# The last weight quarter of a fused attention and FFN kernel in halves, and the first half of its instruction order sought anew

## The chip, the cores and the metric

The kernel runs on one NeuronCore of one Trainium2 chip. The metric is the device time of one execution in microseconds (us). Before the change three executions took 270.04, 270.14 and 270.77; the median is 270.14. Engines are named as in the profile: PE is TensorE (matrix products), DVE is VectorE, ACT is ScalarE, POOL is GpSimd, SP is SyncE, whose queue issues all loads and stores here.

## The reference

Two layers run one behind the other. The first is a linear attention over 8 batches, 8 heads, 576 positions and 64 elements per head, with a cosine and a sine weight by position; the second is a feed-forward layer on its 4608 output rows of 512:

```python
q_p = phi(q, cos_w, sin_w)          # relu(x)*cos and relu(x)*sin, side by side: 128 features
k_p = phi(k, cos_w, sin_w)
kv = np.einsum('bhsf,bhsd->bhfd', k_p, v)
z = np.sum(k_p, axis=2)
num = np.einsum('bhsf,bhfd->bhsd', q_p, kv)
den = np.einsum('bhsf,bhf->bhs', q_p, z)[..., None] + 1e-06
x = (num / den)                     # (8, 8, 576, 64), then to rows of 512
h = x @ w_in                        # 512 -> 2048
g = np.maximum(0.01 * h, h)
out = g @ w_out                     # 2048 -> 512
```

Inputs and output are float32; the kernel computes its products from float16 copies and adds up in float32.

## The kernel before, in words

The 4608 rows are worked off in nine groups of 512: group g (0 to 7) holds the first 512 positions of batch g, group 8 the last 64 positions of all batches. For each batch, VectorE or ScalarE build the weighted parts of k and q (`k_part`, `q_part`; `k_pair` for two heads of batches 0 and 1), cast v to float16 (`v_pair`, `v_main`, `v_tail`; the last 64 columns of each load are ones, so that the product also gives z), TensorE forms kv (`kv_half` for half of the heads in batches 0 and 1, `kv_all` later), an engine copies it out of PSUM, q's parts are transposed (on TensorE with `q_turn` and a copy `q_turned` in batches 0 and 1, by a DMA later), TensorE forms the numerator and denominator (`num_half`, `num`), and `divide` takes a small `den`, a reciprocal and a product. The result x is transposed (`x_turn` and the copy `x_turned` for groups 0 and 1, `x_transpose` for group 2, a DMA later).

The feed-forward layer's first product is plain for groups 0 and 1 (`ffn1`, `quad`, `f1_pair`), and takes seven products of half-size blocks for the others (`p1`), with sums of blocks of the weights (`w1_sums`) and of x (`x_sums`, tile `xw`) made ahead. The second product is plain for group 0 (`ffn2`: 16 matmuls of 512 columns for each of four token tiles, four for each quarter of w2) and takes seven products for the others (`p2`), with sums of w2 (`w2_sums`) and of g (`g_sums`). What the sevens leave in PSUM is put together by `u_copy`, `u_add`, `seed`, `lrelu`, and `o_copy`, `o_add`; `o_store` writes 512 KB out.

The weights come in quarters: `load_w1` and `load_w2` (line 161, 1 MB each for w2) fill staging buffers, `cast_w1` and `cast_w2` (line 570) make float16 copies. The casts and copies go through `copy` (lines 261 to 265), which takes the engine as an argument, so an operation can be on VectorE, ScalarE or GpSimd.

What sets the order: the program is built without a scheduler. Every engine runs its instructions in the order in which the Python code issues them, and waits at the head of its queue for what the next one needs. All loads go through SP's queue in the order of their issue; the same 16 DMA engines serve them. Buffers come from pools of fixed size, and a load into a buffer waits for the last reader of what it held. Up to group 0's second product and group 1's attention the order is written out as calls (lines 599 to 776). The rest are calls handed to `put` (line 1240) with a place from the table `PLACE` (line 1080); the table `ON` gives the engine; the list is sorted by place and called.

Idle matmuls on a blank tile (`idle`) keep TensorE running during the first loads.

Of the kernel before, what the change touches and what calls it, by code (L numbers as in the profile page):

```python
# [9 lines left out]
dt = mybir.dt  # L10
# [4 lines left out]
J = 4  # L15


@with_exitstack
def kernel(
# [62 lines left out]
    st = {"h_turn": 0}  # L82

    def psum(where, shape, dtype, name):
        if where == "h":
            where = f"h{st['h_turn']}"
        if where[0] == "h":
            st["h_turn"] = 1 - int(where[1])
        return ps_of[where[0]].tile(shape, dtype, name=name, tag="ps_" + where)
# [5 lines left out]
    def staged(shape, name, soon=False):  # L95
        p, tag = (early, "early") if soon else (stage, "stage")
        return p.tile(shape, dt.float32, name=name, tag=tag)

    def load_main(nm, src, b, parts=(0, 1), soon=False):

        if parts[0] == 0:
            st[nm, b] = staged([P, H, J, D], f"{nm}st", soon)
        lo, hi = 4 * parts[0], 4 * parts[-1] + 4
        nc.sync.dma_start(
            st[nm, b][:, lo:hi],
            src[b, lo:hi, 0:MAIN, :].rearrange("h (p j) d -> p h j d", j=J),
        )

    def load_kvtail(nm, src, b):

        t = kvtail.tile([P, H // 2, D], dt.float32, name=f"{nm}tl", tag="kvtail")
        v4 = src[b, :, MAIN:S, :].rearrange("(c o) p d -> o p c d", o=2)
        for o in range(2):
            nc.sync.dma_start(t[o * TAIL : (o + 1) * TAIL], v4[o])
        st[nm + "t", b] = t

    def load_qtail(i):
        if "qt" not in st:
            st["qt"] = staged([P, J, H, D], "qtl")
        for o in range(2):  # L120
            nc.sync.dma_start(
                st["qt"][o * TAIL : (o + 1) * TAIL, i],
                q[2 * i + o, :, MAIN:S, :].rearrange("h p d -> p h d"),
            )

    def load_pair(nm, src, b, lo, hi):
# [3 lines left out]
        flat = src[b].rearrange("h s d -> (h s d)").rearrange("(c x e) -> x c e", x=P, e=JP * D)  # L130
# [3 lines left out]

    def load_k(b):
        load_main("k", k, b)
        load_kvtail("k", k, b)

    def load_v(b):
        load_main("v", v, b)  # L140
        load_kvtail("v", v, b)
# [12 lines left out]
    def load_w1(i, cp):  # L154
# [6 lines left out]
    def load_w2(i):  # L161
        t = staged([P, 4, DM], "w2st", i > 1)
        nc.sync.dma_start(t, w2v[i])  # L163
        st["w2", i] = t

    load_main("q", q, 0, (0,))
    load_pair("k", k, 0, 0, 1)
    load_pair("k", k, 0, 1, 2)
    load_main("q", q, 0, (1,))
    load_pair("k", k, 0, 2, 4)  # L170
    load_pair("v", v, 0, 0, 2)
    load_pair("v", v, 0, 2, 4)
    load_w1(0, 0)
    load_w1(1, 0)
    load_w1(0, 1)
    load_w1(1, 1)
    load_w1(3, 0)
    load_w1(3, 1)
    load_w1(2, 0)
    load_w1(2, 1)  # L180

    blank = early.tile([P, MAIN], dt.float16, name="blank", tag="blank", bufs=1)
    nc.vector.memset(blank, 0.0)
    none = const.tile([P, P], dt.float16, name="none")
    nc.gpsimd.memset(none, 0.0)

    def idle(n, where="h1"):
# [4 lines left out]
    idle(11)  # L192

    ident32 = early.tile([P, P], dt.float32, name="ident32", tag="ident32", bufs=1)
    make_identity(nc, ident32)
    ident = const.tile([P, P], dt.float16, name="ident")
    nc.vector.tensor_copy(ident, ident32)
    w_ang = math.pi / 2.0 / S  # L200
    half_pi = const.tile([P, 1], dt.float32, name="half_pi")
    nc.vector.memset(half_pi, math.pi / 2.0)
    eps = const.tile([P, 1], dt.float32, name="eps")
    nc.vector.memset(eps, 1e-6)
    zero = const.tile([P, 1], dt.float32, name="zero")
    nc.vector.memset(zero, 0.0)
    NA = J + 1 + JP
    pos = const.tile([P, NA], dt.float32, name="pos")
    nc.gpsimd.iota(
        pos[:, 0:J],  # L210
        pattern=[[1, J]],
        base=0,
        channel_multiplier=J,
        allow_small_or_imprecise_dtypes=True,
    )
    for o in range(2):
        nc.gpsimd.iota(
            pos[o * TAIL : (o + 1) * TAIL, J : J + 1],
            pattern=[[1, 1]],
            base=MAIN,  # L220
            channel_multiplier=1,
            allow_small_or_imprecise_dtypes=True,
        )
        nc.gpsimd.iota(
            pos[o * TAIL : (o + 1) * TAIL, J + 1 : NA],
            pattern=[[1, JP]],
            base=0,
            channel_multiplier=JP,
            allow_small_or_imprecise_dtypes=True,
        )  # L230
    cos_t = const.tile([P, NA], dt.float32, name="cos_t")
    sin_t = const.tile([P, NA], dt.float32, name="sin_t")
    nc.scalar.activation(cos_t, pos, AF.Sin, bias=half_pi, scale=w_ang)
    nc.scalar.activation(sin_t, pos, AF.Sin, bias=zero, scale=w_ang)
    warm = const.tile([P, 1], dt.float16, name="warm")
    nc.scalar.activation(warm, zero, AF.Lrelu)

    ones = const.tile([P, H, J, 2], dt.float32, name="ones")
    nc.vector.memset(ones, 1.0)
    vmain = const.tile([P, H, J, NE], dt.float16, name="vmain")  # L240
    nc.vector.tensor_copy(vmain[:, :, :, D:NE], ones)
    vtail = const.tile([P, H // 2, 2, NE], dt.float16, name="vtail")
    nc.gpsimd.memset(vtail, 0.0)
    for o in range(2):
        sl = slice(o * TAIL, (o + 1) * TAIL)
# [671 lines left out]
    def f1_all(g):  # L917
# [16 lines left out]
        if sets == 4:  # L934
            return
# [406 lines left out]
```

## Time and profile before

| what | value |
|---|---|
| median of three executions | 270.14 us |
| span of the profiled execution | 268.3 us |
| TensorE busy | 262.5 us, 98% |
| VectorE busy | 209.2 us, 78% |
| ScalarE busy | 198.6 us, 74% |
| GpSimd busy | 7.7 us, 3% |
| bytes moved by DMA | 57.05 MB, mean 213 GB/s |

The total of the profiled execution itself is not given; the median of the others lies 1.84 us above its span. In a list of instructions the columns are start, duration (or the sum, where an entry holds several, "x4"), engine, line, operation, tile written from tiles read, and shapes; in brackets stands the idle time of the engine ahead of the instruction, and what ended it. The duration of a pipelined matmul overlaps with the next, so the pace of TensorE is read from one start to the next. The names of tiles: `qst`, `kst`, `vst`, `kpr`, `vpr`, `w1st`, `w2st` are staging buffers, `xp` and `xs` quotients, `xT` transposed x, `ps_...` PSUM tiles, `u` the sums of the first product, `ob` the output's.

### The profile page before, as it was taken

The page shows a single profiled execution, that of the slowest core. Times are in us where ns is not written, and L with a number is a line of the kernel's source. Part 1 is how long each engine was busy: PE and PEld are TensorE (multiplying, and loading weights), DVE is VectorE, ACT ScalarE, POOL GpSimd, SP SyncE. Part 2 cuts the span into 40 slices and gives each one's busy share as a digit, 9 for nine tenths or more (in the row PEclk, how much of TensorE's full clock was granted, in tenths as well). Part 3 has the DMA queues.
Part 4 walks back from the last instruction along what each step waited for, and adds up shares of the span by engine and source line. Part 5 has one row for each costly group of instructions (what it writes and reads, how often), then busy time and mean ns, then how long its engine had stood idle before and what let it go on. Part 6 is the DMA issues. An engine that isn't in the chain of part 4 may idle for free.

```text
span 268.3 us, 6694 instructions
## 1 busy us (share of the span) xinstructions
PE 262.5 (98%) x2715; PEld 222.9 (83%) x2715; DVE 209.2 (78%) x436; ACT 198.6 (74%) x336; POOL 7.7 (3%) x20
## 2 busy tenths in 40 slices
PE   8999999999999999999999999999999999999994
PEld 3585455566999999999999999999998999999983
DVE  4894998997998998889979967897876674746641
ACT  7675545787989999689878967984996666785621
POOL 2121011000000000000000000000000000000000
PEclk9999999999999999999999999999999999999999
DMA  6999999999999999989899999798893623200116
GB/s 207 377 385 399 380 411 365 276 249 281 209 304 254 234 240 245 264 199 222 221 231 238 198 293 255 140 181 151 135 204 22 138 43 125 112 2 0 78 36 201
DMA packets 82654, 57.05 MB, mean 213 GB/s; under 512 B 54464, under 2 KB 75968, under 8 KB 82112
## 3 DMA queue, kind: packets, MB, share of 16 engines
q1 hardware_dynamic: 82320, 56.37, 84.0%
q8 instruction: 21, 0.34, 0.5%
q10 hardware_dynamic: 304, 0.26, 0.3%
q14 instruction: 9, 0.07, 0.1%
HBM read 36.70 MB, written 9.44 MB: 172 GB/s over the span
## 4 chain that ended last, share of the span: by engine, by line
PE 82%; DMA 13%; SPq 3%; DVE 1%; POOL 0%; issue 0%
PE ps_o L975 34%; PE ps_h L882 18%; PE ps_s L882 14%; DMA w2st<-in_moe_w_out_dram 6%; PE ps_h L833 5%; DMA w1st<-in_moe_w_in_dram 4%; PE ps_num L418 3%; DMA kpr<-in_k_dram 3%; PE ps_kv L317 2%; SPq L131 2%; PE ps_h L975 2%; PE ps_o L543 1%; PE ps_s L975 1%; PE ps_kv L324 1%; DVE w L265 0%; SPq L163 0%
## 5 line engine op out<-in xcount | busy, mean ns | idle before, releaser
L975 PEld LDWEIGHTS <-g 128*128 128x128 f16 x640 | 62.1, 98 | 6.8
L268 DVE TENSOR_TENSOR u<-ps_s,u 128x512 f32<-128x512 f32 x56 | 38.5, 687 | 19.3 <-PE ps_s L882 18.4
L882 PEld LDWEIGHTS <-w 128*128 128x128 f16 x448 | 48.7, 114 | 1.0
L975 PE MATMUL ps_o<-w,g 128*128 128x256 f16 x352 | 46.8, 273 | 0.0
L902 ACT COPY u<-ps_h 128x512 f32<-128x512 f32 x56 | 32.8, 589 | 6.3 <-PE ps_h L882 6.0
L882 PEld LDWEIGHTS <-wa 128*128 128x128 f16 x336 | 34.4, 106 | 1.9
L882 PE MATMUL ps_h<-xw,w 128*128 128x256 f16 x224 | 32.5, 273 | 0.0
L975 PE MATMUL ps_o<-wb,g 128*128 128x256 f16 x232 | 31.5, 273 | 0.0
L909 ACT ACTIVATE g<-u 128x1024 f16<-128x1024 f32 x28 | 29.6, 1060 | 2.3 <-DVE u L268 2.3
L975 PEld LDWEIGHTS <-gs 128*128 128x128 f16 x256 | 24.6, 98 | 2.6
L994 ACT COPY ob<-ps_o 128x512 f32<-128x512 f32 (+1 forms) x32 | 18.0, 561 | 6.0 <-PE ps_o L975 5.8
L892 ACT COPY ps_s<-ps_h 128x512 f32<-128x512 f32 x28 | 16.2, 579 | 6.2 <-PE ps_h L882 5.7
L895 ACT ACTIVATE g<-ps_s 128x512 f16<-128x512 f32 x28 | 16.8, 601 | 5.1 <-PE ps_s L882 4.8
L895 ACT ACTIVATE g<-ps_h 128x512 f16<-128x512 f32 x28 | 16.7, 600 | 5.3 <-PE ps_h L882 5.1
L436 DVE TENSOR_TENSOR xs<-ps_num,rden 128x512 f16<-128x512 f32 x28 | 19.4, 691 | 1.5
L268 DVE TENSOR_TENSOR ob<-ps_o,ob 128x512 f32<-128x512 f32 (+1 forms) x22 | 14.8, 672 | 3.3 <-PE ps_o L975 2.1
L882 PE MATMUL ps_s<-xT,wa 128*128 128x256 f16 x112 | 16.8, 273 | 0.0
L882 PE MATMUL ps_h<-xw,wa 128*128 128x256 f16 x112 | 16.8, 273 | 0.0
L882 PE MATMUL ps_s<-xw,wa 128*128 128x256 f16 x112 | 16.8, 273 | 0.0
L882 PE MATMUL ps_s<-xT,w 128*128 128x256 f16 x112 | 16.8, 273 | 0.0
L882 PE MATMUL ps_h<-xT,w 128*128 128x256 f16 x112 | 16.7, 273 | 0.0
L975 PE MATMUL ps_o<-wb,gs 128*128 128x256 f16 x120 | 16.5, 273 | 0.0
(121 smaller groups left out, 434.5 us busy)
## 6 DMA issues: line engine op xcount, KB each, us to landing
out_dram<-ob SPq DMA_DIRECT2D x16, 512.0 KB, 3.4
qst<-in_q_dram SPq DMA_DIRECT2D x7, 1024.0 KB, 7.0
kst<-in_k_dram SPq DMA_DIRECT2D x6, 1024.0 KB, 8.1
vst<-in_v_dram SPq DMA_DIRECT2D x6, 1024.0 KB, 6.8
w1st<-in_moe_w_in_dram SPq DMA_DIRECT2D x8, 512.0 KB, 11.6
w2st<-in_moe_w_out_dram SPq DMA_DIRECT2D x4, 1024.0 KB, 13.3
vpr<-in_v_dram SPq DMA_DIRECT2D x4, 576.0 KB, 10.7
kpr<-in_k_dram SPq DMA_DIRECT2D x3, 576.0 KB, 11.1
```

The costliest lines, as they stand in the source:

```text
L131: nc.sync.dma_start(st[nm, b][:, lo:hi].rearrange("p c j d -> p c (j d)"), flat[:, lo:hi])
L268: nc.vector.tensor_tensor(out=o, in0=a, in1=b, op=ALU.add)
L418: nc.tensor.matmul(ps[lo:hi, h // 4, (h % 4) * NE : (h % 4) * NE + NM], lhsT=qpT[:, h, lo:hi], rhs=kv[b][:, h, 0:NM],)
L436: nc.vector.tensor_tensor(out=xs, in0=ps[:, :, 0 : 4 * NE].rearrange("p a (b e) -> p a b e", e=NE)[:, :, :, 0:D], in1=rden.rearrange("p (a ...
L833: nc.tensor.matmul(ps, lhsT=w1[m // 4][c // 2][:, c % 2, m % 4 : 512 : 4], rhs=st["xT", g][:, c], start=(c == 0), stop=(c == NKC - 1),)
L882: nc.tensor.matmul(bank[:, p], lhsT=w(c), rhs=x_blocks(g)[n][:, c], start=(fresh and p == 0 and c == 0), stop=(c == 1), skip_group_check=True,
L892: nc.scalar.copy(bank1[bj], bank1[bi])
L895: nc.scalar.activation(st["g" + nm, g][:, 2 * t : 2 * t + 2], bank1[bi], AF.Lrelu)
L902: nc.scalar.copy(st["u", g, t][:, n], bank1[bi])
L909: nc.scalar.activation(st["gt", g][:, :, 1, 2 * t : 2 * t + 2], st["u", g, t], AF.Lrelu)
L975: nc.tensor.matmul(bank, lhsT=st[G2[n], g][:, m, pair * P : (pair + 1) * P], rhs=W2[n](m), start=(fresh and m == 0), stop=(m == NH - 1), s ...
L994: nc.scalar.copy(o_at(g, half_, col, pair), bank_of(bi, pair, pair is None))
```

## The change

The program is now one text, `ORDER`, of 1,518 rows such as `ffn2 0 2 12 14`, which a loop reads from top to bottom: the first word names a function, the others are its arguments, and a letter stands for an engine (A for ScalarE, V for VectorE, G for GpSimd). Functions that did two things are cut in parts (`num_mm`, `den`, `rec`, `xdiv` in place of `num`; `kv_mm` and `kv_copy`; `f1_open`, `f1_mm`, `f1_act`; `xt_mm` and `xt_copy`), so that other rows can stand between. From 98 us or so on, TensorE's order is the one before.

Three things differ up to there. First, w2's last quarter is loaded by two DMAs of half the size, cast in two halves (the first on ScalarE, the second on VectorE), and multiplied in halves for three of the four token tiles. Second, many operations stand elsewhere. Third, some are on another engine: w1's casts are on GpSimd, ScalarE and VectorE in another mix, w2's second quarter is cast by ScalarE, three copies `q_turned` of batch 0, some `x_turned` and `v_pair`, and parts of k and q changed engines. The instructions as a whole (5432 rows on TensorE) are the same in number.

```diff
-    def load_w2(i):
-        t = staged([P, 4, DM], "w2st", i > 1)
-        nc.sync.dma_start(t, w2v[i])
-        st["w2", i] = t
+    def ldw2(i, lo, hi):
+        if lo == 0:
+            st["w2", i] = staged([P, 4, DM], "w2st", i > 1)
+        nc.sync.dma_start(st["w2", i][:, lo:hi], w2v[i][:, lo:hi])
...
-    def ffn2(g, tt, part):
+    def ffn2(g, tt, lo, hi):
         ps = st["ps_o", g, tt]
-        for m in range(4 * part, 4 * part + 4):
+        for m in range(lo, hi):
...
-    def cast_w2(i, eng):
-        copy(eng, w2[:, 4 * i : 4 * i + 4, :], st["w2", i])
+    def cast_w2(i, lo, hi, eng):
+        copy(eng, w2[:, 4 * i + lo : 4 * i + hi, :], st["w2", i][:, lo:hi])
...
+v_pair 1 2 3 G; kv_half 1 1 h1; hrec 1 0 0; hdiv 1 0 0; cast_w2 3 2 4 V; num_half 1 1 0 h0;
+cast_w2 3 0 2 A; kv_half_copy 1 1 A; ffn2 0 2 12 14; hden 1 1 0 A; num_half 1 1 1 h1;
...
-    for _, f, args in sorted(line, key=lambda e: e[0]):
-        f(*args)
+    for n, row in enumerate(ORDER.replace("\n", " ").split(";")):
+        if row.strip():
+            name, *args = row.split()
+            OPS[name](*(int(a) if a.isdigit() else words.get(a, a) for a in args))
```

**VectorE at the first divisions of batch 0 (12 to 16 us).** `kp` are the weighted parts of k, `qpT` copies of q's transposes, `den`, `rden` and `xp` belong to the division. Before:

```order
L282 SCALAR_TENSOR_TENSOR kp<-kpr,cos_t 128x9x64
L282 SCALAR_TENSOR_TENSOR kp<-kpr,sin_t 128x9x64
L265 COPY qpT<-ps_qt 128x512
L282 SCALAR_TENSOR_TENSOR kp<-kpr,cos_t 128x9x64
L282 SCALAR_TENSOR_TENSOR kp<-kpr,sin_t 128x9x64
L433 TENSOR_SCALAR den<-ps_numh 128x8
L435 RECIPROCAL rden<-den 128x8
L436 TENSOR_TENSOR xp<-ps_numh,rden 128x2x256
```

Now:

```order
L508 SCALAR_TENSOR_TENSOR kp<-kpr,cos_t 128x9x64 x2
L508 SCALAR_TENSOR_TENSOR kp<-kpr,sin_t 128x9x64
L491 COPY qpT<-ps_qt 128x512 x2
L508 SCALAR_TENSOR_TENSOR kp<-kpr,sin_t 128x9x64
L491 COPY qpT<-ps_qt 128x512
L666 RECIPROCAL rden<-den 128x8
L670 TENSOR_TENSOR xp<-ps_numh,rden 128x2x256
```

Two copies of q's transposes came to VectorE ahead of the first division, and the first `den` left it for ScalarE.

**SP's queue of loads behind w1.** `w2st` are w2's quarters, `kpr` and `vpr` halves of batch 1's k and v, the first `qst` batch 1's q. Before:

```order
L163 DMA w2st<-in_moe_w_out_dram 128x2048
L104 DMA qst<-in_q_dram 128x8x256
L131 DMA vpr<-in_v_dram 128x2x576
L163 DMA w2st<-in_moe_w_out_dram 128x2048
L131 DMA kpr<-in_k_dram 128x2x576
L131 DMA vpr<-in_v_dram 128x2x576
L163 DMA w2st<-in_moe_w_out_dram 128x2048
L104 DMA qst<-in_q_dram 128x8x256
L104 DMA kst<-in_k_dram 128x8x256
```

Now:

```order
L411 DMA w2st<-in_moe_w_out_dram 128x2048 x2
L359 DMA qst<-in_q_dram 128x8x256
L386 DMA kpr<-in_k_dram 128x2x576
L386 DMA vpr<-in_v_dram 128x2x576
L411 DMA w2st<-in_moe_w_out_dram 128x2048
L386 DMA kpr<-in_k_dram 128x2x576
L386 DMA vpr<-in_v_dram 128x2x576
L411 DMA w2st<-in_moe_w_out_dram 128x1024 x2
L369 DMA vtl<-in_v_dram 64x4x64
L359 DMA kst<-in_k_dram 128x8x256
L359 DMA qst<-in_q_dram 128x8x256
```

The first half of k went behind w2's second quarter and q (before, it stood between w2's first two quarters), the last quarter became two loads, and batch 2's k and q changed places.

**VectorE around the last quotient of batch 2 and the first sums of group 2's x (66 to 72 us).** `xs` are quotients, `gs` and `g` sums of group 1's g, `xw` sums of x, `w` sums of weights, `vtail` casts of v. Before:

```order
L435 RECIPROCAL rden<-den 128x8
L436 TENSOR_TENSOR xs<-ps_num,rden 128x512
L271 TENSOR_TENSOR w_3_0_111<-w_1_0_107,w_3_0_111 128x256x2
L433 TENSOR_SCALAR den<-ps_num 128x8
L435 RECIPROCAL rden<-den 128x8
L436 TENSOR_TENSOR xs<-ps_num,rden 128x512
L271 TENSOR_TENSOR gs_953<-g 128x1024
L271 TENSOR_TENSOR gs_954<-g,gs_953 128x1024 x2
L271 TENSOR_TENSOR xw<-xT 128x512
L271 TENSOR_TENSOR xw<-xT,xw 128x512
```

Now:

```order
L497 TENSOR_TENSOR gs_983<-g 128x1024
L497 TENSOR_TENSOR gs_984<-g,gs_983 128x1024
L662 TENSOR_SCALAR den<-ps_num 128x8
L666 RECIPROCAL rden<-den 128x8
L670 TENSOR_TENSOR xs<-ps_num,rden 128x512
L483 TENSOR_SCALAR qp<-qst,cos_t 128x8x64
L483 TENSOR_SCALAR qp<-qst,sin_t 128x8x64
L494 TENSOR_TENSOR g<-g 128x1024
L483 TENSOR_SCALAR qp<-qst,sin_t 128x8x64
L491 COPY xT<-ps_xt 128x4x128
L497 TENSOR_TENSOR xw<-xT 128x512
L497 TENSOR_TENSOR xw<-xT,xw 128x512
```

Between the last quotient and the first sums of x now stand three parts of batch 3's q, another sum of g and a copy of `xT`, which ScalarE made before; two of the sums of g went ahead of `den`. Batch 3's q is loaded by an issue that now stands behind all four transposes of batch 2's q on SP, and before stood between the second and the third.

1036 lines of the change are left out of this document (436 added, 600 removed), and 52 rows, old and new, of the table PLACE.

## The prediction

> **What bounds the kernel now.** I read the page's busy shares first, then the waits of TensorE, then its rows around every wait, and last the rows of VectorE and ScalarE that end just before them.
>
> ```profile
> PE 262.5 (98%) x2715; PEld 222.9 (83%) x2715; DVE 209.2 (78%) x436; ACT 198.6 (74%) x336; POOL 7.7 (3%) x20
> PE 82%; DMA 13%; SPq 3%; DVE 1%; POOL 0%; issue 0%
> ```
>
> TensorE is busy for 98% of the span, and most of the chain that ended last is TensorE. The amount of its work does not change, so an order can only open or close gaps. By stage:
>
> ```profile
> core 0: us, PE busy (x) PEld busy (x) DVE busy (x) ACT busy (x) POOL busy (x), PEclk, DMA share, GB/s
> 16.70:50.50 33.80, 33.66 (x309) 20.44 (x307) 27.83 (x51) 18.94 (x27) 3.08 (x3) 1.00 1.06 379
> ...
> 70.00:80.00 10.00, 10.00 (x117) 9.38 (x115) 9.94 (x22) 8.96 (x17) 0.00 (x0) 1.00 1.02 274
> ```
>
> Granted clock 1.00 in both stretches (the column behind the engines). From 16.7 to 50.5 us TensorE is busy 33.66 of 33.80, so behind 16.7 almost nothing is left to win; between 70 and 80 us VectorE is busy 9.94 of 10 us, as full as TensorE. What TensorE waits for, by its rows (an entry's start minus the one before, against its matmuls' own pace):
>
> ```profile
> 12.67 0.51 PE L349 MATMUL ps_kvh<-vpair,kp 64*128 64x65 f16 x21 [0.42 <-POOL vpair L265]
> ...
> 15.61 0.40 PE L475 MATMUL ps_xth<-ident,xp 128*128 128x128 f16 x4 [0.37 <-DVE xp L436]
> ...
> 45.26 0.42 PE L453 MATMUL ps_numh<-kv,qpT 128*128 128x65 f16 x8
> 45.83 0.59 PE L543 MATMUL ps_o<-w,g 128*128 128x512 f16 x2
> ...
> 76.85 0.60 PE L975 MATMUL ps_o<-wb,gs 128*128 128x256 f16 x4
> 77.29 0.60 PE L975 MATMUL ps_o<-wb,g 128*128 128x256 f16 x4
> 77.85 0.60 PE L882 MATMUL ps_h<-xT,w 128*128 128x256 f16 x4
> ```
>
> There are four gaps: 0.42 at 12.67, 0.37 at 15.61, 0.31 before 45.83 (eight matmuls of 65 columns go at 0.26, as 67.20 to 67.46 below, so the next was due at 45.52), and 0.12 before 77.85 (0.56 after 77.29 where 0.44 lies between 76.85 and 77.29). Together 1.22 us, 0.45% of the time: that is nearly all that any order can win here.
>
> **Part 1, the first divisions.** The second `q_turned` of pair 2 stands on VectorE ahead of the first reciprocal and that of pair 1 in front of the last `k_pair`; the first `hden` goes to ScalarE.
>
> ```profile
> 12.29 0.42 DVE L265 COPY qpT<-ps_qt 128x512 f16<-128x512 f16 x1 [0.19 <-PE ps_qt L405]
> 12.63 0.75 DVE L282 SCALAR_TENSOR_TENSOR kp<-kpr,cos_t 128x576 f16<-128x576 f32 x1
> 13.29 1.21 DVE L282 SCALAR_TENSOR_TENSOR kp<-kpr,sin_t 128x576 f16<-128x576 f32 x1
> 14.43 0.15 DVE L433 TENSOR_SCALAR den<-ps_numh 128x8 f32<-128x8 f32 x1
> 14.62 0.20 DVE L435 RECIPROCAL rden<-den 128x8 f32<-128x8 f32 x1
> 14.86 0.69 DVE L436 TENSOR_TENSOR xp<-ps_numh,rden 128x512 f16<-128x512 f32 x1
> ...
> 13.20 0.70 POOL L265 CAST vpair<-vpr 128x576 f16<-128x576 f32 x1 [0.58 <-DMA vpr<-in_v_dram]
> ```
>
> One copy more ahead of the `k_pair` (0.34 from one start to the next, 12.29 to 12.63) uses up the 0.19 that VectorE waited and a little more; the copy behind it replaces the 0.19 of `hden` (14.43 to 14.62). The division then starts 0.15 later, and the transposes at 15.61 with it: +0.15. The bounds are 0, if the stretched `k_pair` takes the extra copy (its 1.21 ends with the GpSimd cast at 13.90, not with its own start), and 0.34 + 0.34 − 0.19 − 0.19 = 0.30. The gap at 12.67 stays: what stands before it is the same on every engine.
>
> **Part 2, w2's last quarter in halves.**
>
> ```profile
> 29.64 14.88 DMA w2st<-in_moe_w_out_dram
> 44.55 1.24 DVE w L265
> ...
> 73.78 0.69 DVE L265 CAST vmain<-vst 128x1024 f16<-128x1024 f32 x1
> ...
> L909 ACT ACTIVATE g<-u 128x1024 f16<-128x1024 f32 x28 | 29.6, 1060 | 2.3 <-DVE u L268 2.3
> ```
>
> The chain of waits shows the transfer, then the cast of 1.24, and its end at 45.79 is what the products at 45.83 wait for. The bytes queued ahead are the same, so the second half lands at 44.5 too and the first 0.52 MB / 379 GB/s = 1.38 earlier, at 43.2. ScalarE casts the first (1.06 by its nearest row, done at 44.3), VectorE the second (0.69, done at 45.25). TensorE wants the first at 45.4 to 45.5 and the second two more steps later: the gap goes, −0.31. Bounds: −0.31, and 0 if something else (VectorE's `hdiv` ahead of the cast) is late by as much. The extra issue on SP lies behind the queue of loads. The other moves up to 50 us (casts of w1 to GpSimd, `x_turned` to VectorE, w2's second quarter to ScalarE) I cost at nothing: VectorE had 27.83 and ScalarE 18.94 busy of 33.80. If that cover fails, one late cast costs at most its own 1.0.
>
> **Part 3, the small gap at 77.85** comes from the order of rows around it, which is another now: −0.12, or 0.
>
> **Part 4, VectorE from 67 to 82 us.** Between 50 and 100 us VectorE gets an estimated 2 us more work and ScalarE some 3.7 less (the instructions that the two orders give each engine, counted by kind, times durations as in the rows here: copies of xT at 0.42, parts of k and q at 0.48, casts of v at 0.69). Where `num` 2 2 and the sums of group 2's x stood early, they now come behind more work:
>
> ```profile
> 67.20 0.42 PE L418 MATMUL ps_num<-kv,qpT 128*128 128x65 f16 x8
> 67.46 0.60 PE L975 MATMUL ps_o<-w,g 128*128 128x256 f16 x4
> ...
> 72.48 0.60 PE L882 MATMUL ps_h<-xw,wa 128*128 128x256 f16 x4
> ...
> 79.98 0.60 PE L975 MATMUL ps_o<-w,gs 128*128 128x256 f16 x4
> ...
> 64.94 0.48 DVE L257 TENSOR_SCALAR qp<-qst,sin_t 128x512 f16<-128x512 f32 x1
> 65.33 0.48 DVE L257 TENSOR_SCALAR qp<-qst,cos_t 128x512 f16<-128x512 f32 x1
> 67.66 0.17 DVE L433 TENSOR_SCALAR den<-ps_num 128x8 f32<-128x8 f32 x1 [0.32 <-PE ps_num L418]
> 68.10 0.69 DVE L436 TENSOR_TENSOR xs<-ps_num,rden 128x512 f16<-128x512 f32 x1
> 68.70 0.68 DVE L271 TENSOR_TENSOR gs<-g 128x1024 f16<-128x1024 f16 x1
> 69.30 1.28 DVE L271 TENSOR_TENSOR gs<-g,gs 128x1024 f16<-128x1024 f16 x2
> 70.96 0.42 DVE L271 TENSOR_TENSOR xw<-xT,xw 128x512 f16<-128x512 f16 x1
> 77.62 0.68 DVE L271 TENSOR_TENSOR w<-w 128x1024 f16<-128x1024 f16 x1
> ```
>
> Before, the second sum of x ended at 71.38, 1.10 ahead of its product at 72.48. In the new order `num` 2 2 stands one product step (0.44) later but 0.2 is saved by then, so `den` starts at 67.66 + 0.44 − 0.2 = 67.9. To the end of the second sum VectorE then has, start to start: `den` and reciprocal 0.44 (67.66 to 68.10), division 0.60 (to 68.70), three parts of q at 0.40 (64.94 to 65.33), one sum of g at 0.60 (68.70 to 69.30), the copy of xT 0.4, two sums of x 0.85 (0.42 twice): 4.1, so 72.0. TensorE reaches the product two steps earlier than before relative to `num` (5.28 − 0.87 = 4.4 behind 67.44, 71.85): a stall of 0.2. From there to `w2_sums` 0 3, which ended at 78.3 before, the new order has nineteen VectorE instructions of 0.3 to 0.6 pitch, together 9.0: it runs from 80.9 to 81.6, and its product, at 79.98 before and two steps (0.87) later now, is due at 80.9 plus some 0.35 of shifts and stalls so far, and waits 0.3 with the handover. Three shorter handovers (`g_sums` 1 1 4 8, `u_add`, group 3's x) I put at 0.25 together. Sum +0.75. Bounds: 0, if VectorE keeps pace through reorderings that I have not seen, and 1.7, if of the 2 us that VectorE gets only its one wait here (0.32 at 67.66) takes any in.
>
> **Sum.** +0.15 − 0.31 − 0.12 + 0.75 = +0.47. The span of 268.3 becomes 268.8. What lies around the span is 1.84 (the median of 270.14 minus it; the profiled execution's own total is not shown), which I leave: 270.6. About 0.3%, 0.8 us, is what a measurement of this kernel tells from no change; the whole sum is inside it.
>
> **A rule against the change.** The stretched `k_pair` has a brother in this order's busiest hand-over:
>
> ```profile
> 39.73 1.43 DVE L282 SCALAR_TENSOR_TENSOR kp<-kpr,cos_t 128x576 f16<-128x576 f32 x2
> 41.07 1.89 DVE L282 SCALAR_TENSOR_TENSOR kp<-kpr,sin_t 128x576 f16<-128x576 f32 x2
> ...
> 41.31 1.04 POOL L265 CAST vpair<-vpr 128x576 f16<-128x576 f32 x1 [4.49 <-ACT qpT L263]
> ```
>
> Two `k_pair`s take 1.43, and 1.89 beside a GpSimd cast, which itself takes 1.04 instead of 0.70. The change gives GpSimd two such casts in a row. By the rows they end at 41.31 + 2 × 1.04 = 43.4 and VectorE loses 2 × 0.46; `kv_half` 1 1 wants both at about 44.3. It belongs to the third rival below. The Trainium skill's page "SBUF — State Buffer", section "Who interferes with whom", says that an instruction of VectorE with two inputs in SBUF and a GpSimd instruction that reads SBUF lock each other out for the whole instruction. The trace agrees (both are longer when they overlap). By it, with strict turns of 0.67 and 0.70, the second cast would end at 43.9, still 0.4 ahead, so the sum by it is the same, and this rival's chance is 0.07 in place of the 0.03 that the rows alone would leave it.
>
> **The rivals.**
>
> First, slower: the load of q for batch 3 becomes the wait. Before, SP issued it at 55.30; now it stands behind the transposes of q and takes the buffer of v's batch 2, free when its cast ends at about 58.4.
>
> ```profile
> 56.19 5.74 SPq L386 DMA_TRANSPOSE qpT<-qp  x2
> ...
> qst<-in_q_dram SPq DMA_DIRECT2D x7, 1024.0 KB, 7.0
> ```
>
> If the issue comes when those two transposes ended before, at 61.9, it lands at 68.9 with the median of 7.0. VectorE's first part of q 3 starts at 67.9 + 0.44 + 0.60 = 68.95. From a landing after 68.95 on, each microsecond holds VectorE's queue, with the sums of x behind it, and so TensorE. At 8 us instead of 7 it costs 0.95 more: 271.6. Against it: the transposes may issue earlier, when their q parts are earlier.
>
> Second, no loss: VectorE catches up in part 4, because the waits fall where TensorE has other work first. Then +0.15 − 0.31 − 0.12 = −0.28, 269.9; with the start's gap of 0.37 closed too, 269.3. For it speaks that ScalarE is relieved by more than VectorE gets; against it VectorE's 9.94 of 10.
>
> Third, slower: k and v of batch 1 come late. k's first half is now queued behind w2's second quarter and q (two loads of 1.05 MB, 2.77 each at 379 GB/s), so it lands 5.5 later, and all four first `k_pair`s and a cast of v that VectorE takes from GpSimd stand between that and `kv_half` 1 0; the two GpSimd casts stand before `kv_half` 1 1. It decides when the casts of v end later than by the rows by 0.9 (by strict turns 0.4); one cast too late is 0.70 on the path, 271.3. Against it: v itself lands where it did, and ScalarE has room.
>
> That the halves do nothing is a case of the second bound of part 2: 0.31 more, 270.9.
>
> **How the numbers follow.** Forecast (stalls of 0.4 to 1.2 in part 4): 0.42, of which 0.08 lies above 270.95. Late q or a queue on VectorE beyond that: 0.24, all slower. No loss: 0.27, of which 0.10 is below 269.33. Late k and v: 0.07, slower. So faster 0.10, same 0.34 + 0.17 = 0.51, slower 0.39. The predicted time is 270.6. The range reaches from 269.4 (the second rival with one more gap closed) to 271.9 (the first rival with part 4 at its bound).
>
> **What would show it.** Right: no idle time before the products with w2's last quarter near 45.5, x's transposes at 15.7 to 15.8, a gap of 0.2 before group 2's sixth product at 72 and one of 0.3 near 81, both released by VectorE. Wrong: a VectorE wait on `qst` near 69, a `ps_kvh` wait on `kp` or `vpair` at 38 or 44, or VectorE idle from 67 to 82 with no wait of TensorE on it.

## The result: 3.5 us slower, and the profile after

The changed kernel takes 273.62 us (median of six executions, 273.42 to 276.0); the kernel before, on the same chips, 270.09. The ratio is 1.0136, with a 95% interval of 1.0109 to 1.0163. The forecast was 270.6, in a range of 269.4 to 271.9: the result lies outside it. Two executions further below (278.56 and 280.39), taken while the chip ran slower at a lower clock, are left out of the medians there.

The page's busy shares, and the waits of TensorE by line (in total, times, longest):

```profile
PE 264.1 (97%) x2715; PEld 222.8 (82%) x2715; DVE 206.7 (76%) x431; ACT 200.7 (74%) x340; POOL 12.1 (4%) x22
```

```profile
PE ps_kvh L575 <- POOL vpair L491: 1.1, 1, 1.1
PE ps_h L943 <- DMA xT<-xs: 0.7, 1, 0.7
PE ps_xth L715 <- DVE xp L670: 0.5, 1, 0.5
PE ps_h L943 <- DVE xw L497: 0.3, 1, 0.3
PE ps_o L1009 <- DVE w L497: 0.2, 1, 0.2
```

The first line stood at 0.4 before, the third at 0.4, the others were not there. Where the time is lost is read from TensorE's rows for work that both orders reach at a like point: the first product of batch 4's kv, before and after.

```profile
101.52 0.42 PE L317 MATMUL ps_kv<-vmain,kp 128*128 128x65 f16 x8
```

```profile
104.91 0.42 PE L545 MATMUL ps_kv<-vmain,kp 128*128 128x65 f16 x8
```

It is 3.39 later, and the span is longer by 3.3 (271.6 against 268.3): all of the loss lies ahead of 105 us, where the two orders differ, and nothing is lost or won behind. The first product of batch 2's kv divides it, since both orders give TensorE the same matmuls ahead of it, and the same between the two marks:

```profile
59.12 0.42 PE L317 MATMUL ps_kv<-vmain,kp 128*128 128x65 f16 x8
```

```profile
60.35 0.61 PE L545 MATMUL ps_kv<-vmain,kp 128*128 128x65 f16 x8
```

So 1.23 is lost ahead of 59 us and 2.16 from there on (42.40 before, 44.56 now). In the order of time, in the rows of the same profile:

**The first products (0.76, chance).** The 19 idle products at the start took, before and after:

```profile
1.19 6.49 PE L190 MATMUL ps_idle<-blank 128*128 128x512 f16 x19 [1.19 <-DVE blank L183]
```

```profile
1.19 7.25 PE L416 MATMUL ps_idle<-blank 128*128 128x512 f16 x19 [1.19 <-DVE blank L438]
```

They are the same instructions at the same start; they run at half pace at first (0.43 from start to start, 0.22 later), and the change to full pace came later. This is no part of the change (more below). It is in this pair of profiles, and need not be in other executions.

**GpSimd's cast of the first v (0.66).** GpSimd's and VectorE's rows there, and the product that waits:

```profile
11.23 3.41 POOL L491 CAST vpair<-vpr 128x576 f16<-128x576 f32 x2 [8.52 <-DMA vpr<-in_v_dram]
```

```profile
11.42 1.42 DVE L508 SCALAR_TENSOR_TENSOR kp<-kpr,cos_t 128x576 f16<-128x576 f32 x2
12.76 0.75 DVE L508 SCALAR_TENSOR_TENSOR kp<-kpr,sin_t 128x576 f16<-128x576 f32 x1
13.43 0.75 DVE L491 COPY qpT<-ps_qt 128x512 f16<-128x512 f16 x2
```

```profile
14.09 0.74 PE L575 MATMUL ps_kvh<-vpair,kp 64*128 64x65 f16 x36 [1.07 <-POOL vpair L491]
```

Two casts took 3.41, of which the first alone 2.80; before they took 0.91 and 0.70. Three `k_pair`s now stand in one piece on VectorE, from 11.42 to 13.5, and the cast that began at 11.23 did not come through until the copies from PSUM began. The Trainium skill's page "SBUF — State Buffer", section "Who interferes with whom", states this: VectorE with two inputs in SBUF and GpSimd reading SBUF lock each other out, and who is first blocks the other. The rows agree with the lock; of who comes first they show something else, since the cast began 0.19 ahead of the three and was held off all the same. The prediction cited the rule, and applied it at 41 us and not here. `kv_half` 0 0 begins 1.42 later, 0.76 of it from the idle products.

**w2's halves.** The gap ahead of the last quarter is gone, as forecast: behind the eight matmuls of 65 columns comes the next after 0.26 each time (46.51 to 46.77, 47.20 to 47.46).

```profile
46.51 0.43 PE L687 MATMUL ps_numh<-kv,qpT 128*128 128x65 f16 x8
46.77 0.59 PE L783 MATMUL ps_o<-w,g 128*128 128x512 f16 x2
47.20 0.42 PE L687 MATMUL ps_numh<-kv,qpT 128*128 128x65 f16 x8
47.46 1.02 PE L783 MATMUL ps_o<-w,g 128*128 128x512 f16 x4
```

The wait at the first division grew by 0.09. The changes ahead of 59 us then add up to 0.76 + 0.66 + 0.09 − 0.31 = 1.20 of the 1.23.

**VectorE from 69 to 84 us.** `den` of batch 2's last quotient starts at 69.68 and the second sum of x at 73.49; its product starts at 73.97, 0.89 behind the one before it, where 0.44 is the pace. The other wait of the kind stands at 83.53, for `w2_sums` 0 3: the product of 130 columns ahead of it started at 83.12 and takes 0.06 (82.49 to 82.55), so 0.35 is lost.

```profile
69.68 0.16 DVE L662 TENSOR_SCALAR den<-ps_num 128x8 f32<-128x8 f32 x1
...
73.49 0.42 DVE L497 TENSOR_TENSOR xw<-xT,xw 128x512 f16<-128x512 f16 x1
```

```profile
73.08 0.60 PE L943 MATMUL ps_s<-xT,w 128*128 128x256 f16 x4
73.97 0.60 PE L943 MATMUL ps_h<-xw,wa 128*128 128x256 f16 x4 [0.30 <-DVE xw L497]
...
83.12 0.22 PE L552 MATMUL ps_kv<-vtail,kp 128*128 128x130 f16 x1
83.53 0.72 PE L1009 MATMUL ps_o<-w,gs 128*128 128x256 f16 x5 [0.19 <-DVE w L497]
```

**The transposes of group 3's x.** The chain of waits at 92.64 and the product behind it: 1.27 from 97.76 to 99.03 where 0.44 is the pace, 0.83 lost.

```profile
92.64 6.25 DMA xT<-xs
```

```profile
97.76 0.60 PE L1009 MATMUL ps_o<-w,g 128*128 128x256 f16 x4
99.03 0.60 PE L943 MATMUL ps_h<-xT,w 128*128 128x256 f16 x4 [0.67 <-DMA xT<-xs]
```

SP's issues ahead of it, and before's:

```profile
64.39 0.53 SPq L359 DMA_DIRECT2D qst<-in_q_dram  x1
...
81.42 6.00 SPq L608 DMA_TRANSPOSE qpT<-qp  x2
87.46 1.29 SPq L369 DMA_DIRECT2D vtl<-in_v_dram  x2
88.79 0.61 SPq L359 DMA_DIRECT2D vst<-in_v_dram  x1
89.93 6.63 SPq L619 DMA_TRANSPOSE xT<-xs  x4
```

```profile
83.79 0.50 SPq L104 DMA_DIRECT2D vst<-in_v_dram  x1
84.33 1.61 SPq L114 DMA_DIRECT2D vtl<-in_v_dram  x2
86.47 2.54 SPq L397 DMA_TRANSPOSE xT<-xs  x2
```

Batch 3's q is loaded at 64.39 (55.30 before), batch 4's v at 88.79 (83.79), 1.1 ahead of the first transposition, where it was 2.7 ahead. SP's queue shows no idle time from 81.42 to 88.79: v's load comes behind two transposes of batch 3's q and v's own last rows. The stages show what the two engines do meanwhile:

```profile
60.00:70.00 10.00, 9.98 (x120) 6.96 (x119) 8.29 (x21) 6.11 (x9) 0.00 (x0) 1.00 0.83 242
70.00:80.00 10.00, 9.70 (x90) 8.61 (x88) 9.83 (x22) 8.17 (x15) 0.00 (x0) 1.00 1.15 281
80.00:90.00 10.00, 9.81 (x127) 9.24 (x125) 9.69 (x24) 9.29 (x18) 0.00 (x0) 1.00 1.10 248
```

Columns as in the prediction: ScalarE is busy 6.11 of 10 us from 60 to 70 (8.31 before), where it used to make batch 3's parts of q. That work comes later, into a stretch where VectorE is full (9.83 from 70 to 80, and 9.69 from 80 to 90, 8.67 there before). That the late q is the reason is argued from these rows, not shown by a run.

The gaps named here and two small ones (0.19 at 60.63, 0.20 at 103.60), less the 0.13 that stood before 77.85, make 0.19 + 0.45 + 0.35 + 0.83 + 0.20 − 0.13 = 1.89 of the 2.16; the rest is in gaps too small to read one by one.

### The profile page after: what moved, and what is told of

Same layout as the page of the kernel before. It is cut to its first block, busy times and chain, and to the rows that moved or that the text cites. A ratio compares the mean times of both kernels' runs of the same rounds, so it can differ in the third digit from the quotient of the medians.

```text
span 271.6 us, 6698 instructions
## 1 busy us (share of the span) xinstructions
PE 264.1 (97%) x2715; PEld 222.8 (82%) x2715; DVE 206.7 (76%) x431; ACT 200.7 (74%) x340; POOL 12.1 (4%) x22
## 4 chain that ended last, share of the span: by engine, by line
PE 86%; DMA 5%; DVE 4%; POOL 1%; SPq 1%; ACT 1%; issue 0%; DVEq 0%
PE ps_o L1009 31%; PE ps_h L943 16%; PE ps_s L943 12%; PE ps_o L783 5%; PE ps_h L900 5%; PE ps_h L746 4%; DMA vpr<-in_v_dram 3%; PE ps_num L640 3%; DMA xT<-xs 2%; PE ps_kv L545 2%; PE ps_h L1009 2%; PE ps_s L1009 1%; PE ps_hq L765 1%; POOL vpair L491 1%; PE ps_xth L715 1%; PE ps_kvh L575 1%
```

## The experiments

Times are medians; the kernel before took 270.1 to 270.4 beside them. TensorE's waits of each run are those of its profile.

**The same two kernels again, for a second profile.**

> The changed kernel as it is, for a second profile. What an order does comes again: TensorE waits at 14, 74, 83.5 and 99. What is chance differs: the half-speed stretch of the first idle products, which ended at 6.4 in the first profile and at 5.2 in that of before.

Two executions took 273.59 and 274.25. All the waits come again, that for v's casts with 1.1 as before; the one for x's transposes changes much (the waits of TensorE; total, times, longest):

```profile
PE ps_h L943 <- DMA xT<-xs: 1.9, 1, 1.9
```

> The kernel before as it is, for a second profile: the end of the half-speed stretch at the start, near 5.2 again if the kernel sets it, anywhere from 4 to 7 if chance does; the gaps of 0.42 and 0.37 at the start and of 0.31 at 45.8 come again.

270.50 (269.74 to 271.19). The first idle product at full pace began at 4.91 in this profile (5.35 in the first of this kernel; 7.19 and 5.82 in the two of the changed kernel). The wait for v's casts was 0.8 here (0.4 in the first), the wait at 15.6 came again, and in place of the gap at 45.8 there is one of 0.8 at 19.9 for a cast of w1 on ScalarE. So a delay ahead of 45 us and w2's gap can replace each other: a TensorE that comes later does not wait there.

These two profiles divide the loss otherwise than the first two: batch 2's kv begins at 59.85 in the changed kernel and at 59.76 in the kernel before, batch 4's at 105.74 and 102.04. Here nearly all of the 3.7 us lies behind 59 us (45.89 against 42.28).

**One row at the start.** In the changed kernel one `k_pair` goes behind the two copies of q:

```diff
-k_pair 0 2 0; k_pair 0 2 1; q_turned 0 1 4 8 V; q_turned 0 0 4 8 V; k_pair 0 3 1;
+k_pair 0 2 1; q_turned 0 1 4 8 V; q_turned 0 0 4 8 V; k_pair 0 2 0; k_pair 0 3 1;
```

> The changed kernel with one row moved: VectorE's `k_pair` 0 2 0 goes back behind the two copies of q's transposes, so that two and no longer three of these run back to back while GpSimd casts the first v. Theory (VectorE and GpSimd shut each other out): the cast ends about 0.5 us sooner (13.5 in place of 14.0 in a profile with the same start) and the kernel takes 273.1. Rival (the cast waits for v, or GpSimd is slow for its own reasons): the cast still takes 2.8 and the time stays 273.6.

273.47 (271.82 to 274.26; ratio to before 1.0112, 1.0088 to 1.0136). GpSimd's first cast took 0.90, and the wait for it fell from 1.1 to 0.6; the time does not show it clear of its own spread, since x's transposes cost 1.1 in this run. Batch 2's kv begins at 59.21 in this profile, level with the kernel before (59.12), and batch 4's at 104.15 in place of 101.52: what is left of the loss lies behind 59 us. GpSimd's row:

```profile
11.99 0.90 POOL L487 CAST vpair<-vpr 128x576 f16<-128x576 f32 x1 [9.29 <-DMA vpr<-in_v_dram]
```

The reverse, in the kernel before:

```diff
-    q_turned(0, 0, 4, 8, DVE)
-    q_turned(0, 1, 4, 8, ACT)
-    q_turn(0, 3, 4, 8, "o")
     k_pair(0, 2, 0)
+    q_turned(0, 0, 4, 8, DVE)
+    q_turned(0, 1, 4, 8, ACT)
+    q_turn(0, 3, 4, 8, "o")
```

> The kernel before with one call moved: `k_pair` 0 2 0 on VectorE ahead of the copies of q's transposes, so that three such instructions run back to back beside GpSimd's cast of the first v. Theory (VectorE and GpSimd shut each other out): the cast takes 1.5 to 2.2 in place of 0.91, `kv_half` 0 0 starts 0.5 to 0.9 later, 270.7 to 270.9. Rival (the cast waits for v's landing only): 0.9 as before, 270.1.

270.91 against 270.11 (ratio 1.0027, 1.0015 to 1.0039). The two casts took 2.56 (the first 1.42) in place of 0.91 and 0.70, `kv_half` waited 1.1. So the wait follows the call in both kernels. Over all the profiles of this document it is 0.4 to 0.8 in the nine with this call behind the copies, and 1.1 to 1.9 in the eleven with it ahead of them. The price in time is some 0.7 us by the ratio (0.4 to 1.1), and it is not paid each time: the profiled execution took 270.04 with the wait in it and began batch 2's kv at 59.19 (59.12 in the kernel before), since the gap at 45.8 is gone there. Four of the twelve executions, 271.15 to 271.34, had a mean granted clock of 0.994. GpSimd's row there:

```profile
11.71 2.56 POOL L265 CAST vpair<-vpr 128x576 f16<-128x576 f32 x2 [9.00 <-DMA vpr<-in_v_dram]
```

**w2's halves alone**, in the kernel before (load in two, first half cast on ScalarE, second on VectorE):

```diff
-        nc.sync.dma_start(t, w2v[i])
+        for n in range(0, 4, 2 if i == 3 else 4):
+            m = n + (2 if i == 3 else 4)
+            nc.sync.dma_start(t[:, n:m], w2v[i][:, n:m])
...
-    cast_w2(3, DVE)
+    cast_w2(3, DVE, 2, 4)
...
+    cast_w2(3, ACT, 0, 2)
     kv_half_copy(1, 1, ACT)
```

> The kernel before with nothing but w2's last quarter loaded and cast in halves (the first on ScalarE, the second on VectorE). Theory: the gap of 0.31 ahead of the products at 45.8 goes, 269.8. Rival (the second load or the cast on ScalarE costs as much as it wins): 270.1 or more.

270.07 against 270.11 (ratio 1.0002, 0.9988 to 1.0017): no gain is seen, though the interval, from 0.3 faster to 0.5 slower, just reaches the 0.31. The gap at 45.8 is gone, and one has come 1.6 us earlier, for `num_half` 1 1 0:

```profile
44.23 0.43 PE L455 MATMUL ps_numh<-kv,qpT 128*128 128x65 f16 x8 [0.16 <-DVE xp L438]
```

TensorE arrives there earlier than its operands: batch 1's attention was next in line behind the weights.

**Single waits of the late part.** Three edits of the changed kernel: batch 4's v loaded ahead of the last transposition of batch 3's q; a sum of g and two parts of q behind the sums they held up on VectorE; all three with the row at the start.

```diff
-q_transpose_dma 3 0; q_transpose_dma 3 3; ldt v 4 0; ...; ldt v 4 1; ld v 4 0 8;
+q_transpose_dma 3 0; ldt v 4 0; ldt v 4 1; ld v 4 0 8; q_transpose_dma 3 3; ...
```

> The changed kernel with the loads of batch 4's v moved ahead of the last transposition of batch 3's q on SP. Theory (these 1.1 MB stand right ahead of the transposes of group 3's x on the DMA engines): v lands near 91, the transposes land 1 to 2 us sooner, TensorE's wait of 0.83 at 99.0 goes to 0.0 to 0.2, 272.8. Rival (the transposes are late because VectorE's quotients are): the wait stays above 0.5, 273.5.

274.65 (ratio 1.0169, 1.0150 to 1.0189), no gain and rather a loss beside the changed kernel (1.0136, 1.0109 to 1.0163; the intervals touch). Batch 3's last heads now wait for their q, whose transposition stood behind v's megabyte:

```profile
95.77 0.43 PE L636 MATMUL ps_num<-kv,qpT 128*128 128x65 f16 x8 [2.92 <-DMA qpT<-qp]
```

```diff
-g_sums 1 1 0 4; q_transpose_dma 3 1; q_part 3 0 1 0 8 V; xt_copy 2 2 V; x_sums 2 1; x_sums 2 2;
+q_transpose_dma 3 1; xt_copy 2 2 V; x_sums 2 1; x_sums 2 2; g_sums 1 1 0 4; q_part 3 0 1 0 8 V;
...
-q_part 3 3 0 0 8 V; u_add 2 0 0 3; w2_sums 0 3;
+u_add 2 0 0 3; w2_sums 0 3; q_part 3 3 0 0 8 V;
```

> The changed kernel with one sum of g and one part of q moved behind the second sum of group 2's x on VectorE, and one part of q behind w2_sums 0 3. Theory (VectorE's queue holds back the sums): the wait at 74.0 (0.46) goes and that at 83.5 (0.35) falls to 0.0 to 0.3, 273.0. Rival (VectorE has no room at all there, so what is taken from one wait comes back at the next handover): the sum of TensorE's gaps from 60 to 90 us stays within 0.2, 273.5.

274.09 (ratio 1.0139, 1.0111 to 1.0167). The waits at 74 and 83 are gone and others have come, for a sum of g, for ScalarE, and for transposes of q at 112. From 62 to 90 us TensorE's gaps above 0.15 add up to 0.75, where the changed kernel has 0.80:

```profile
PE ps_num L636 <- DMA qpT<-qp: 1.3, 1, 1.3
...
PE ps_s L939 <- ACT ps_s L949: 0.3, 1, 0.3
PE ps_o L1005 <- DVE g L490: 0.2, 1, 0.2
```

> The three edits together. If the three causes are independent, the gains add up: 273.6 - 0.5 - 0.8 - 0.6 = 271.7. If one wait stands for the other, 272.3 or more. If it stays above 273, the loss is elsewhere, in the start of the profile (0.75) above all.

274.59 (272.83 to 276.57): nothing adds up; the wait for q's transposition (2.7) replaces that for x's. The rival of the second edit holds in these runs: a wait that is taken away there is found at a later handover.

**The load ahead of x's transposes.** Three runs more: the last parts of batch 3's q made early, so that its buffer is free for v; only half of v ahead of the transposes; the first with q of batch 3 loaded ahead of two transposes.

```diff
-q_part 3 3 0 0 8 V; ... q_part 3 3 1 0 8 A; q_transpose_dma 3 0; q_transpose_dma 3 3; ...
+q_part 3 3 0 0 8 A; o_copy 1 0 0 0; ... q_part 3 3 1 0 8 A; lrelu 2 11 0 2; ...
+q_transpose_dma 3 3; q_transpose_dma 3 0; ldt v 3 0; ... ld q 4 0 8; ldt v 4 0; ldt v 4 1; ld v 4 0 8;
```

> The changed kernel with the two parts of q 3 3 (the last heads of batch 3) made by ScalarE near 71.5 and 73 us in place of 81.8 and 85.4, so that q's buffer comes free, and batch 4's v is loaded, before the transposes of group 3's x are issued. Theory (v's load is late because its buffer is, and stands ahead of those transposes): v is issued near 81.5 in place of 88.8, the transposes land by 97, TensorE's wait of 0.8 to 2.1 at 99 is below 0.3, 272.4. Rival (the transposes wait for VectorE's quotients, or the DMA engines are full whatever the order): the wait stays, 273.5.

273.57 (ratio 1.0127, 1.0110 to 1.0144). The wait for x's transposes is gone, though v went out at 87.0, not at 81.5, because three transposes of q held SP's queue from 71.3 to 77.8. The time has not changed, since 0.4 for a cast of v, 0.2 for ScalarE and others have come.

```diff
-ldt v 4 1; ld v 4 0 8; ... x_transpose_dma 3 3; ... v_main 4 4 8 V; ... v_main 4 0 4 V;
+ldt v 4 1; ld v 4 0 4; ... x_transpose_dma 3 3; ld v 4 4 8; ... v_main 4 0 4 V; ... v_main 4 4 8 V;
```

> The changed kernel with only the first half of batch 4's v loaded ahead of the transposes of group 3's x and the second half behind them (VectorE casts them in that order). Theory (bytes ahead of the transposes): half a megabyte less is 1.5 to 2 us less, the wait at 99 is below 0.4, at the price of at most 0.5 for VectorE at the second cast, 272.7. Rival (the transposes are late for another reason): the wait stays, 273.5 or more.

274.28 (ratio 1.0146, 1.0129 to 1.0162). Again the wait for the transposes is gone, though SP issued the load and the first transposition as before (88.76 and 89.89), so the bytes ahead of them are one cause of it. In the run above the whole megabyte stood 1.1 ahead of them and the wait was gone too: they were issued 1.9 earlier (88.06), and TensorE came to their product 0.9 later (99.14, due at 98.20 in the changed kernel). So the moment of issue counts as well. VectorE now waits for the second half and TensorE for VectorE, dearer than allowed for:

```profile
PE ps_h L939 <- DVE xw L493: 1.6, 2, 1.4
```

```diff
-q_transpose_dma 2 0; q_transpose_dma 2 2; ld q 3 0 8;
+ld q 3 0 8; q_transpose_dma 2 0; q_transpose_dma 2 2;
```

> As the run with the two parts of q 3 3 early, and the load of batch 3's q issued ahead of two transposes of batch 2's q, near 60.3 in place of 64.4 us. Theory: q lands near 66 in place of 70.5, which takes the load of all of batch 3 and 4 off the time near 90; VectorE's first part of q 3, only 0.25 behind the landing now, has room: 272.2 or 0.2 below the other run. Rival (the lateness of this load costs nothing by itself, since VectorE reaches the part only at 70.7): the same time as the other run.

276.15 (273.4 to 276.83), against both theories: q went out at 59.37, and the transposes behind it were so late that batch 2's numerator waited 3.2 at 69. Behind that wait TensorE's granted clock was 0.50 for 3.42 us in this profile, which adds to the loss; two executions with a mean clock of 0.997 and 1.0 took 273.4 and 274.4, four with 0.991 to 0.993 took 276.0 to 276.8.

```profile
59.37 0.38 SPq L355 DMA_DIRECT2D qst<-in_q_dram  x1
60.66 7.45 SPq L604 DMA_TRANSPOSE qpT<-qp  x2
```

```profile
69.64:73.06 3.42, 3.42 (x18) 1.86 (x15) 2.35 (x5) 1.61 (x2) 0.00 (x0) 0.50 0.91 288
```

In the kernel before the same was tried the other way round, with v's place in the table moved:

```diff
-31, 96, 81, 122, 174, 181, 229,
+31, 96, 81, 122, 174, 186.5, 229,
```

> The kernel before with the load of batch 4's v moved on SP's queue from ahead of the transposes of group 3's x to behind the first of them. Theory (a megabyte ahead of a transpose delays it by what it takes to move): the second transpose lands 2 to 4 us later, TensorE waits that long less the 0.2 it has, near 93, 272 to 274. Rival (the transposes go their own way beside the load): 270.1.

270.40 against 270.13 (ratio 1.0011, 1.0000 to 1.0023): the expectation missed. v went out only 1.6 later (85.4), since the transposition that it was moved behind itself went out earlier, and TensorE waited for no transposition. The order before has room there.

**The two orders cut and joined.** Since single waits only moved, both orders were cut at 51 us (end of group 0's second product) and at 68 us (opening of group 1's) and joined crosswise: the rows of the one up to the cut, then those rows of the other that are not yet done.

> The changed kernel's order up to the end of group 0's second product (51 us, with w2's halves, the new loads and the new engines), and from there the order of the kernel before. Theory (nearly all of the loss lies between 51 and 102 us, where both orders differ in VectorE's, ScalarE's and SP's work): 270.0 to 270.8. Rival (the first part sets the lateness, by its loads and the start): 272 or more.

> The order of the kernel before up to 51 us, and from there the changed kernel's. Theory: the loss is all here, 273 to 274, with TensorE waits of 0.3 to 0.5 at 73 and 83 and one for a DMA transposition near 99. Rival: 271 or less.

> The changed order up to the opening of group 1's second product (68 us), then the order before. By the theory that batch 3's loads, issued 3 to 9 us later between 55 and 66 us, leave ScalarE idle there and overfull later, the loss comes again although the order after 68 us is the old one: 272 to 275. Rival (the loss is in the order after 68 us, sums of x and late parts of q): 270.5 or less.

> The order before up to the opening of group 1's second product (68 us), then the changed one. By the theory of the late loads: batch 3's q, v and k land where they landed before, the waits at 83 and 99 go, 270.1 to 271. Rival (the order after 68 us): 272.5 or more.

| order up to the cut | behind it | median | of it a wait at the join |
|---|---|---|---|
| changed, to 51 us | before | 272.32 | 1.0, a leaky ReLU on ScalarE at 56 us |
| before, to 51 us | changed | 275.98 | 1.9, the same at 57 and 59 us |
| changed, to 68 us | before | 275.00 | 2.4, batch 2's last quotient at 73 us |
| before, to 68 us | changed | 272.80 | 0.9, the same at 70 us |

By the medians alone the first expectation missed (272.32 in place of 270.0 to 270.8), because the joins have waits of their own. With these taken off the times are 271.3, 274.1, 272.6 and 271.9 (an estimate, since a wait taken off may come back elsewhere). The profiles need no such estimate for the cut at 51 us: the join's waits lie ahead of batch 2's kv, so the stretch from there to batch 4's kv can be read as it is. First the changed order up to 51 us and the old one behind, then the reverse:

```profile
61.44 0.42 PE L540 MATMUL ps_kv<-vmain,kp 128*128 128x65 f16 x8
...
103.72 0.42 PE L540 MATMUL ps_kv<-vmain,kp 128*128 128x65 f16 x8
```

```profile
62.27 0.42 PE L541 MATMUL ps_kv<-vmain,kp 128*128 128x65 f16 x8
...
106.83 0.42 PE L541 MATMUL ps_kv<-vmain,kp 128*128 128x65 f16 x8
```

The old order behind the cut takes 42.28, as in the kernel before (42.40, and 42.28 in its second profile), although the changed order stands ahead of it; the changed order takes 44.56, as in the changed kernel, although the old order stands ahead of it. So these 2.2 us belong to the order behind 51 us, whatever is ahead. Its waits come again there (for x's transposes 0.9, for sums on VectorE 0.3 and 0.2), and one more at 112 for a transposition of q.

The cut at 68 us divides less. With the old order up to 68 us, the changed one behind has no wait at 83, and at 97 one of 0.2 for ScalarE in place of 0.7 to 1.9 for the transposes. The same stretch takes 44.32, or 43.3 without the join's gap of 1.03, so 0.9 of the 2.2 is left. With the changed order up to 68 us and the old one behind there is one large wait at the join, 2.4, and no other; whether it comes from the late loads or from the join itself this run does not say.

**What the first part costs by itself.** Two runs more with the join at 51 us: batch 2's q loaded ahead of its k, and the row at the start moved as well.

> The changed order up to 51 us, then the order before, as in the run that joined them so, but batch 2's q loaded ahead of its k as in the kernel before. That join cost TensorE a wait of 1.15 at 56 us for a leaky ReLU, behind four parts of q on ScalarE. Theory (those parts waited for q, and the first part of the changed order costs nothing more than its start): that wait falls below 0.3, 271.0 to 271.4. Rival: it stays, 272.3.

> The same with `k_pair` 0 2 0 behind the copies of q's transposes. Theory (VectorE and GpSimd shut each other out): the wait of 1.9 for v's casts near 13 falls to 0.6 to 0.9, 270.0 to 270.7, level with the kernel before. Rival: the rest of the order up to 51 us costs by itself, 271 or more.

272.31 and 271.80 (ratio 1.0056, 1.0035 to 1.0077). The wait at the join stayed at 1.0 both times, so it wasn't q's load; the wait for v's casts fell to 0.4 in the second, but that at the first division rose to 0.7:

```profile
PE ps_xth L710 <- DVE xp L665: 0.7, 1, 0.7
PE ps_kvh L570 <- POOL vpair L486: 0.4, 1, 0.4
```

Without the join's 1.0 this is 270.8, about 0.6 above the kernel before beside it (270.21). No run was faster than the kernel before, clear of noise.

## Why the prediction was wrong

- **Part 4, +0.75** is the step that failed by most. It named two places, group 2's product at 72 and `w2_sums` 0 3 near 81, with stalls of 0.2 and 0.3; they came at 74 and 83.5 with 0.45 and 0.35, so the mechanism was right there and the first size too small. But its working ended at 82 us, although the two orders differ up to 98, and so it put everything behind at nothing without a reason. The wait for the transposes of group 3's x at 99 was 0.83 in the first profile and 2.07 in the second. In all, the stretch from batch 2's kv to batch 4's grew by 2.16 and by 3.61 us in the two pairs of profiles, above the bound of 1.7.
- **"The gap at 12.67 stays: what stands before it is the same on every engine."** This sentence is the second failed step. VectorE's list is the same up to the fourth `k_pair`, but the cast on which the gap depends runs beside the three that follow, and one of those had moved. Its price is 0.66 in the first pair of profiles and some 0.7 by the run with that call moved alone. The rule was in the text, with a row of the same place (13.29, 1.21 beside the cast) ahead of it.
- **Part 1's term** (+0.15 at the first division) came near the wait there, which grew from 0.37 to 0.46, but by luck: VectorE was not held back by the copies. It waited 0.43 for the `den` that had gone to ScalarE, a step that was booked as a relief.

```profile
16.05 0.20 DVE L666 RECIPROCAL rden<-den 128x8 f32<-128x8 f32 x1 [0.43 <-ACT den L660]
```

- **Part 2 and 3** (−0.31 and −0.12): both gaps went. But −0.31 was booked as a gain of the time, and the run with the halves alone shows none: TensorE, freed there, waits 1.6 us earlier. The failed step is "the gap goes, −0.31"; the bound of 0 given beside it fits what was measured (−0.04, with an interval from −0.3 to +0.5).
- **The first rival** (late q of batch 3) named a load that was indeed late, later than in it, issued at 64.39 in place of 61.9. Yet it did not hold up VectorE at 69, which reached its part at 70.72 without idle time. ScalarE's work from 60 to 70 us came later, into the full stretch behind it, and batch 4's v went out 1.1 ahead of the transposes of x; TensorE's wait stood 30 us further on, at 99. That the late q caused these is argued, not shown.
- **The second rival** (no loss) did not hold. **The third** (late k and v of batch 1) did not happen: TensorE has no wait for `kp` or `vpair` near 38 or 44. The rule that was weighed for it, at 41 us, did not decide there.
- **The range** ended at 271.9 because each part was bounded by itself, and none reached behind 82 us. In the runs here, waits that were taken away behind 60 us came back at later handovers, and transposes issued right behind a load of a megabyte cost TensorE 0.8 to 3.2 us.

Open: how the 2.2 to 3.6 us behind 51 us divide between the late loads and the order of VectorE's work. That ScalarE's idle time from 60 to 70 us is the common root is argued from the stages, not shown by a run that mends it alone. What the order up to 51 us costs, 1.1 us by the joined run of 272.31 less its join's 1.0, falls to 0.6 with the call beside GpSimd's cast moved (271.80); where the 0.6 comes from is open. The late start of full pace, 0.76 in the first pair of profiles, is chance and cannot carry the 3.5, since all six executions of the changed kernel (273.42 and more) lie above all six of the kernel before (270.77 and less).

## What to carry to other kernels

When an order is changed, list for each engine what runs beside every cast of GpSimd, and for SP what stands within a few microseconds ahead of every transposition; these are waits that no engine's own list shows. Carry the working on to where the two orders are the same again, 98 us here, and not to the last wait that was thought of. Two marks on the bounding engine with the same work between them, as the two kv products here, show in which stretch a loss lies, also in kernels joined from two orders. Where two engines are both full for tens of microseconds, expect a single wait that is taken away to come back. A gap on the bounding engine is worth its length only if nothing else arrives at the same time behind it; take it away alone in the old kernel before booking it.

## What the hardware showed that was not expected

- The idle products at the start took 6.49 in the first profile and 7.25 in that of the changed kernel, with the same instructions and starts, while the clock row of the profile's page reads full speed in both (the trace holds no record of the clock before 5.26 and 7.02 us, and that row counts this as full). This is not the change's doing: over all the profiles, which share these products, the first record of full clock stands anywhere from 3.9 to 7.0 us. The Trainium skill's page "TensorE: Matmul & The Clock Gate", section "Part 1: The HAM clock gate (the "warmup" mystery)", says that the clock is raised by a window that runs freely and does not start with the kernel; the rows agree with that. That page of the Trainium skill gives a spread of 500 ns to either side; here the measured one is 3.1 us in all.
- One GpSimd cast of 0.70 was held off for 2.1 us by three VectorE instructions of 0.75 in a row (2.80 in the first profile of the changed kernel, 1.76 in the second, 0.90 with one of the three moved). How long depends on when v lands among them: with the same order and a cast that began at 12.50 it took 1.07.
- Two transposes issued 1.3 us behind a load of 1 MB kept SP's queue 7.45 us, and TensorE waited 3.2 for what they brought; two in the changed kernel took 6.00 (at 81.42, behind q's load at 80.98), and two ahead of such a load 2.66 (at 61.64).
- A wait of TensorE can cost more than its length. In the profile with the wait of 3.2 at 69 us the granted clock was 0.50 for 3.42 us behind it, and so for 3.41 us behind waits of 1.8 and 1.9 at 13 us in two of the joined kernels. It does not always follow: the wait of 2.9 at 96 us, in the run with v moved ahead, had none in its profile.
